# One attention-and-two-MLPs kernel: x2 added in its load buffers, the cosine's turns taken as integers, the second weights started earlier, and a new planned order

## The chip, the cores and the metric

The kernel runs on one core of a Trainium2 chip. The metric is the time of one execution on the device in microseconds (us). One execution of the kernel before was recorded by the hardware profiler; every row shown below is of that execution. TensorE is called PE here, its weight loads PEld, VectorE DVE, ScalarE ACT, GpSimd POOL, and SP is the engine whose queue issues every DMA of this kernel.

## The reference

Windowed attention (4 batches, 8 heads, 576 tokens, head size 64; half of the heads see the last 32 keys, half see 32 keys at a distance of 4) is followed by two MLPs on the 2304 tokens of 512 features:

```python
x = attn_out.transpose(0, 2, 1, 3).reshape(2304, 512)
h = x @ w_in                    # 512 -> 2048
x2 = (h * np.cos(h)) @ w_out    # 2048 -> 512
gate = 1 / (1 + np.exp(-(x2 @ w_gate)))   # 512 -> 1536
out = (gate * (x2 @ w_val)) @ w_out2      # 1536 -> 512
```

Weights of the MLPs arrive as 64-bit floats and are taken apart on the chip. Each matrix product is made of three matmuls of a high and a low part in fp32r.

## The kernel before

**Stages.** Attention (12 groups of 192 tokens) runs first, and MLP 1 is woven into it. MLP 1 works in 96 steps: 6 chunks of 384 tokens by 8 blocks of the hidden size for the first half of the hidden size (steps 0 to 47), then the 6 chunks by the other 8 blocks (steps 48 to 95). MLP 2 works in 36 sections: 3 pairs of chunks by 12 blocks; a section is seven products `p(n, j)` (a scheme that saves one product in eight) and six output groups `o(n, i)`. MLP 2's weights are prepared once, written to DRAM (`wd2`, `od2`), and loaded again for each section, so its first pair of chunks runs while later weights are still being prepared.

**One step of MLP 1.** PE makes h in PSUM (12 matmuls, L676 to L678). `turn` (ACT, L725) computes u = h/2pi + 1/4, `whole` (DVE, L729) rounds u to r by adding and subtracting a large number, `part` (DVE, L732) takes u - r, `cosine` (ACT, L735) is the sine of that times 2pi, `g` (DVE, L738) multiplies with h and frees h's PSUM buffer (there are two), `g_hi` (L743 on DVE or L745 on ACT) and `g_lo` (DVE, L748) split the product, and 12 matmuls add it to four accumulators `acc`.

**x2.** At the end of a chunk's first half the four accumulators go to DRAM (`x2h`); at the end of its second half `x2_load` (L797) brings each back into a buffer `xr` (two of them), `take` (DVE, L803) adds the accumulator into a buffer `o` (two of them), and `x2_save` (L817) writes it (`x2d`). In MLP 2 the sums `u2`, `u3` (DVE, L998) also live in `o`; `u2` must be there before product 3 of its section, `u3` before product 5, and `keep` (ACT, L995) before product 2.

**Weights.** `w_tasks(i)` for the 68 weight blocks: load (SP), `low` (ACT, L330), `mag` (L334 on DVE, L338 on ACT for the first 16 blocks), `clamp`, `shift`, `top`, `rnd` (DVE), then high and low parts; blocks i >= 32 are those of MLP 2. `block_tasks` makes `th` (ACT, L429; one buffer), which is free again once `w2_save` (L437) has landed in `wd`. L965 loads it back. There are two `raw` and two `wc` buffers for weights in work.

**What sets the order.** `Plan.run` is a list scheduler that runs at build time: each task has an engine, an assumed duration, a priority, tasks that it needs, buffers that it takes and gives, and for DMAs an assumed latency `lat` (ns) until the data are there. What it finds is written out as the program, and on the chip every engine and the SP queue work through their instructions strictly in that order. A `gate` keeps a load from being placed before PE has reached a step. [...]

Of the kernel before, what the change touches and what calls it, by code (L numbers as in the profile page):

```python
# [22 lines left out]
NEG = -(2.0**33)  # L23
MAGIC = 1.5 * 2.0**23
INV_2PI = 0.15915494309189535
TWO_PI_DOWN = 6.2831850051879883
F64_MIN = 2.0**-15
# [11 lines left out]
W_PRIO, W_START = 4.5, -4  # L39
W_GATE = (4.413, 1.646, 1.612)  # L40
XS_LEAD = (15.0, 0.6)
# [6 lines left out]
class Plan:  # L48
# [129 lines left out]
def windowed_attention_mlp_kernel(ctx, tc, q, k, v, w_in, w_out, w_gate, w_val, w_out2, out):  # L178
# [128 lines left out]
    def w_tasks(i):  # L307
# [401 lines left out]
    def mlp_tasks(n):  # L709
# [13 lines left out]
        def turn():  # L723
            st["u"] = gp.tile([P, CH], F32, tag="u", name="u")
# [6 lines left out]
        def part():  # L731
# [24 lines left out]
        for kk in range(KD):  # L756
# [9 lines left out]
        add(("turn", n), "act", 460, turn, [("h", n, KD - 1)], p - URGENT, take=["u"])  # L766
        add(("whole", n), "dve", 270, whole, [("turn", n)], p - URGENT, take=["r"], port=True)
        add(("part", n), "dve", 470, part, [("whole", n)], p - URGENT, give=["r"], port=True)
        add(("cos", n), "act", 415, cosine, [("part", n)], p - URGENT, table="trig")
# [22 lines left out]
    def x2_out(s, c, half, n, i):  # L792
        st = {}

        def load():
            st["r"] = gp.tile([P, CH], F32, tag="xr", name="xr")
            SP.dma_start(out=st["r"], in_=x2h[c][:, i, :])  # L797

        def take():
            st["o"] = gp.tile([P, CH], F32, tag="o", name="o")  # L800
            ps = acc_t[s, i][:, :CH]
            if half:
                DVE.tensor_tensor(out=st["o"], in0=ps, in1=st["r"], op=ALU.add)  # L803
            elif i % 2:
                DVE.tensor_copy(st["o"], ps)
            else:
                ACT.activation(out=st["o"], in_=ps, func=AF.Copy)

        p = n + 2.0
        deps = [("x2", n, i)]  # L810
        if half:
            add(("x2_load", s, i), "sp", 550, load, [("x2_save", order.index(c), i)], p - 4, take=["xr"], lat=2200,
                after=xr_prev("x2_load", s, i))
            deps.append(("x2_load", s, i))
        add(("x2_take", s, i), "dve" if half or i % 2 else "act", 470, take, deps, p, take=["o"],
            give=["acc"] + (["xr"] if half else []))
        add(("x2_save", s, i), "sp", 550, lambda: SP.dma_start(out=(x2d if half else x2h)[c][:, i, :], in_=st["o"]),  # L817
            [("x2_take", s, i)], p, give=["o"], lat=2200)

# [11 lines left out]
    def xs_tasks(s):  # L831
# [7 lines left out]
        for kk in range(2):  # L839
# [18 lines left out]
            def key(what, nm):  # L858
                return (what, s, kk, nm)
# [4 lines left out]
            for i, nm in enumerate(("b0", "b1", "a0", "a1")):  # L864
                c, k = (2 * s if nm[0] == "a" else 2 * s + 1), 2 * int(nm[1]) + kk
                deps = [("x2_save", NC + c, k), "late"]
                add(key("xs_load", nm), "sp", 550, lambda nm=nm, f=load: f(nm), deps, base - 1 + i * 0.01, take=["xt"], lat=2200, gate=gate,
                    after=prev + ([key("xs_load", ("b0", "b1", "a0")[i - 1])] if i else []))
# [21 lines left out]
    def xs_wide(s, ca, cb):  # L890
# [67 lines left out]
    def mlp2_tasks(n):  # L958
# [196 lines left out]
```

## Time and profile before

| what | value |
|---|---|
| median of 3 runs | 1016.99 us (1014.67 to 1018.88) |
| the profiled execution | 1018.92 us |
| its span, first to last instruction | 1017.0 us |
| PE busy, DVE busy, ACT busy | 962.0, 726.4, 473.5 us |
| weight loads of PE busy | 898.8 us |
| mean granted clock of PE | 0.98 |

The span is the part of an execution in which instructions run; 1.9 us lie around it. Busy times overlap, since the engines work side by side. Matmuls are pipelined, so PE counts as busy also where its matmuls follow each other more slowly than they could.

### The profile page before, as it was taken

What the parts mean: (1) busy time and instruction counts of PE and PEld (TensorE: products, weight loads), DVE (VectorE), ACT (ScalarE), POOL (GpSimd) and SP (SyncE); (2) the same over time, 40 slices, a digit from 0 to 9 for tenths busy, and PEclk for the clock granted to TensorE, in tenths of its full rate; (3) what the DMA queues carried; (4) which work ended last, traced back from release to release, by engine and by line L of the source; (5) the groups of instructions that cost most, each with busy time, mean ns of one, the idle gap of its engine ahead of it and who ended that gap; (6) DMA issues with size and microseconds to landing.
All of it is one profiled execution on the core that took longest, in us unless ns stands there. A gap on an engine that the chain in (4) does not pass through costs nothing.

```text
span 1017.0 us, 16393 instructions
## 1 busy us (share of the span) xinstructions
PE 962.0 (95%) x6007; PEld 898.8 (88%) x6007; DVE 726.4 (71%) x1543; ACT 473.5 (47%) x1165; POOL 184.3 (18%) x227
## 2 busy tenths in 40 slices
PE   7889999999999999999998979989999999999996
PEld 6778789898999999989998968879999999999995
DVE  7799898989865588889999777766644545543443
ACT  5768778777664254544564523332322213322112
POOL 6324333323111022222112222220000000000000
PEclk9689999999999999999999999989999999999999
DMA  7564555454310228768647889888454643644441
GB/s 185 140 183 132 170 142 175 136 168 122 77 52 7 73 88 297 272 218 280 256 178 248 295 320 341 300 309 311 175 182 171 243 151 145 212 170 186 147 145 62
DMA packets 107759, 189.80 MB, mean 187 GB/s; under 512 B 56992, under 2 KB 91040, under 8 KB 100512
## 3 DMA queue, kind: packets, MB, share of 16 engines
q1 hardware_dynamic: 107680, 188.77, 54.9%
q8 instruction: 47, 0.77, 0.3%
q14 instruction: 32, 0.26, 0.1%
HBM read 139.98 MB, written 48.76 MB: 186 GB/s over the span
## 4 chain that ended last, share of the span: by engine, by line
PE 64%; DVE 17%; DMA 10%; ACT 7%; issue 2%; SPq 0%; POOL 0%; DVEq 0%; ACTq 0%; POOLq 0%
PE oacc L1066 4%; PE oacc L1067 4%; PE oacc L1065 4%; PE acc L676 4%; PE ps_h L676 4%; PE ps_h L678 4%; PE ps_h L677 4%; PE acc L678 4%; PE acc L677 4%; PE ps_y L986 3%; PE ps_y L988 3%; PE ps_y L987 3%; DMA wd<-th 2%; PE ps_z L988 2%; PE ps_z L987 2%; PE ps_x L986 2%
## 5 line engine op out<-in xcount | busy, mean ns | idle before, releaser
L676 PE MATMUL ps_h<-arena 128*128 128x384 f32 x384 | 134.0, 349 | 5.6 <-DVE u L738 5.6
L676 PE MATMUL acc<-gs,arena 128*128 128x384 f32 x384 | 135.3, 352 | 3.8 <-DVE o L803 3.6
L678 PE MATMUL ps_h<-arena 128*128 128x384 f32 x384 | 129.7, 338 | 0.0
L677 PE MATMUL ps_h<-arena 128*128 128x384 f32 x384 | 129.7, 338 | 0.0
L678 PE MATMUL acc<-gs,arena 128*128 128x384 f32 x384 | 128.8, 335 | 0.0
L677 PE MATMUL acc<-gs,arena 128*128 128x384 f32 x384 | 128.6, 335 | 0.0
L998 DVE TENSOR_TENSOR u<-ps_y,s 128x384 f32<-128x384 f32 x72 | 39.9, 554 | 87.1 <-PE ps_y L988 80.6
L434 POOL TENSOR_TENSOR th<-tb,th 128x512 fp32r<-128x512 f32 (+1 forms) x48 | 63.6, 1343 | 211.6 <-ACT th L429 211.6
L725 ACT ACTIVATE u<-ps_h,q 128x384 f32<-128x384 f32 x96 | 55.3, 576 | 69.8 <-PE ps_h L678 51.1
L1065 PE MATMUL oacc<-arena 128*128 128x512 f32 x216 | 85.5, 396 | 2.2 <-DVE arena L1027 2.2
L1067 PE MATMUL oacc<-arena 128*128 128x512 f32 x216 | 86.5, 400 | 0.0
L1066 PE MATMUL oacc<-arena 128*128 128x512 f32 x216 | 86.4, 400 | 0.0
L676 PEld LDWEIGHTS ps_h<-arena 128*128 128x128 f32 x384 | 73.1, 190 | 9.1 <-DVE u L738 8.2
L1013 ACT ACTIVATE sg<-sg 128x384 f32<-128x384 f32 x36 | 18.8, 523 | 133.7 <-DVE sg L1009 133.7
L986 PE MATMUL ps_y<-arena 128*128 128x384 f32 x216 | 73.6, 341 | 7.3 <-DVE u L998 6.8
L676 PEld LDWEIGHTS acc<-gs,arena 128*128 128x128 f32 x384 | 72.2, 188 | 6.6 <-DVE o L803 5.3
L677 PEld LDWEIGHTS ps_h<-arena 128*128 128x128 f32 x384 | 73.2, 191 | 0.0
L988 PE MATMUL ps_y<-arena 128*128 128x384 f32 x216 | 73.1, 338 | 0.0
L987 PE MATMUL ps_y<-arena 128*128 128x384 f32 x216 | 73.1, 338 | 0.0
L678 PEld LDWEIGHTS ps_h<-arena 128*128 128x128 f32 x384 | 73.0, 190 | 0.0
L677 PEld LDWEIGHTS acc<-gs,arena 128*128 128x128 f32 x384 | 72.3, 188 | 0.0
L678 PEld LDWEIGHTS acc<-gs,arena 128*128 128x128 f32 x384 | 72.1, 188 | 0.0
(135 smaller groups left out, 2341.6 us busy)
## 6 DMA issues: line engine op xcount, KB each, us to landing
arena<-wd SPq DMA_DIRECT2D x36, 1792.0 KB, 7.4
wd<-th SPq DMA_DIRECT2D x12, 1792.0 KB, 8.4
wst<-in_moe_w_out_dram SPq DMA_DIRECT2D x28, 512.0 KB, 4.8
wst<-in_moe_w_in_dram SPq DMA_DIRECT2D x16, 512.0 KB, 4.2
xd<-arena SPq DMA_DIRECT2D x4, 1536.0 KB, 6.8
wst<-in_moe_w_gate_dram SPq DMA_DIRECT2D x12, 512.0 KB, 5.8
wst<-in_moe_w_val_dram SPq DMA_DIRECT2D x12, 512.0 KB, 4.4
arena<-xd SPq DMA_DIRECT2D x4, 1536.0 KB, 8.2
```

Source lines behind the costliest of these rows:

```text
L434: POOL.tensor_tensor(out=t[:, 1, c], in0=wf[f][:, c].bitcast(F32), in1=t[:, 0, c].bitcast(F32), op=ALU.subtract)
L676: PE.matmul(ps, wh, xl, start=first, stop=False)
L677: PE.matmul(ps, wl, xh, start=False, stop=False)
L678: PE.matmul(ps, wh, xh, start=False, stop=last)
L725: ACT.activation(out=st["u"], in_=st["h"], func=AF.Identity, scale=INV_2PI, bias=q25)
L986: PE.matmul(st[to], wh, xl, start=first, stop=False, **more)
L987: PE.matmul(st[to], wl, xh, start=False, stop=False, **more)
L988: PE.matmul(st[to], wh, xh, start=False, stop=kk == 1, **more)
L998: DVE.tensor_tensor(out=tile_of(nm, tag), in0=st[ps], in1=st[other], op=ALU.add)
L1065: PE.matmul(ps, ul, w[:, 0, :], start=f == 0, stop=False)
L1066: PE.matmul(ps, uh, w[:, 1, :], start=False, stop=False)
L1067: PE.matmul(ps, uh, w[:, 0, :], start=False, stop=f == F2 - 1)
```

## The change

- **The turns.** `turn` writes r as 32-bit integers straight from ACT; `whole` is gone; `part` is one scalar_tensor_tensor that reads h from PSUM again: u = h * (1/2pi) - r. The quarter turn moves to `cosine`, which now has a bias tile `half_pi`.
- **x2 in place.** `x2_load` of second-half chunks goes to `xr` for columns 0 and 1 and to `o` for columns 2 and 3 (all four to `xr` in the last chunk); `take` adds the accumulator into that same buffer, which is free again when the save has landed.
- **MLP 2.** `u3` uses the second half of the gate tile `sg`, `va` overwrites `u2`.
- **Weights.** MLP 2's loads may start at step 36 with 1.7 steps between them (before: 48 and 1.612). `mag` of every weight may go to ACT.
- **Assumed latencies** of weight, x2, xs, xw, `w2` and `o2` DMAs are longer.

```diff
-W_GATE = (4.413, 1.646, 1.612)
+W_GATE = (4.413, 1.646, 36.0, 1.7)
...
-            gate = min(NC * FN[0] + j * W_GATE[2], need - 8)
-        add(("w_load", i), "sp", 1460, load, [], pr - 2 if j + 2 * F1 >= 2 * FN[0] else GS * (i / 4 - 6) + W_START, take=["raw"], lat=2200, gate=gate,
+            gate = min(W_GATE[2] + j * W_GATE[3], need - 8)
+        add(("w_load", i), "sp", 1460, load, [], pr - 2 if j + 2 * F1 >= 2 * FN[0] else GS * (i / 4 - 6) + W_START, take=["raw"], lat=2200 if i < 2 * FN[0] else 3200, gate=gate,
...
-            alt=("act", 520, mag_act, False) if i < 2 * FN[0] else None)
+            alt=("act", 520, mag_act, False))
...
-        add(("o2_save", f), "sp", 1460, save, [("w_lo", i)], pr + 0.5, give=["oh"], lat=2200)
-        add(("w", key), "sp", 1460, load, [("o2_save", f), last_use(old)], NSTEP + SEC * f - 1.0, lat=2200)
+        add(("o2_save", f), "sp", 1460, save, [("w_lo", i)], pr + 0.5, give=["oh"], lat=6000)
+        add(("w", key), "sp", 1460, load, [("o2_save", f), last_use(old)], NSTEP + SEC * f - 1.0, lat=4500)
...
-        add(("w2_save", f), "sp", 4400, save, done, pr, give=["th"], lat=2200)
+        add(("w2_save", f), "sp", 5400, save, done, pr, give=["th"], lat=3500)
...
         def turn():
-            st["u"] = gp.tile([P, CH], F32, tag="u", name="u")
-            ACT.activation(out=st["u"], in_=st["h"], func=AF.Identity, scale=INV_2PI, bias=q25)
-
-        def whole():
-            st["r"] = gp.tile([P, CH], F32, tag="r", name="r", bufs=1)
-            DVE.tensor_scalar(st["r"], st["u"], MAGIC, -MAGIC, op0=ALU.add, op1=ALU.add)
+            st["r"] = gp.tile([P, CH], I32, tag="r", name="r", bufs=1)
+            ACT.activation(out=st["r"], in_=st["h"], func=AF.Identity, scale=INV_2PI, bias=q25)
 
         def part():
-            DVE.tensor_tensor(out=st["u"], in0=st["u"], in1=st["r"], op=ALU.subtract)
+            st["u"] = gp.tile([P, CH], F32, tag="u", name="u")
+            DVE.scalar_tensor_tensor(st["u"], st["h"], INV_2PI, st["r"], op0=ALU.mult, op1=ALU.subtract)
 
         def cosine():
-            ACT.activation(out=st["u"], in_=st["u"], func=AF.Sin, scale=TWO_PI_DOWN)
+            ACT.activation(out=st["u"], in_=st["u"], func=AF.Sin, scale=TWO_PI, bias=half_pi)
...
+        tag = "xr" if half and (i < 2 or s == 2 * NC - 1) else "o"
         def load():
-            st["r"] = gp.tile([P, CH], F32, tag="xr", name="xr")
-            SP.dma_start(out=st["r"], in_=x2h[c][:, i, :])
+            st["o"] = gp.tile([P, CH], F32, tag=tag, name=tag)
+            SP.dma_start(out=st["o"], in_=x2h[c][:, i, :])
 
         def take():
...
-                DVE.tensor_tensor(out=st["o"], in0=ps, in1=st["r"], op=ALU.add)
+                DVE.tensor_tensor(out=st["o"], in0=ps, in1=st["o"], op=ALU.add)
...
-        add(("u3", n), "dve", 560, lambda: plus("u3", "o", "y", "s1"), [("p", n, 3, 1), ("u2", n)], u, take=["o"])
-        add(("vb", n), "dve", 560, lambda: plus("vb", "u", "z", "u3"), [("p", n, 4, 1), ("u3", n)], u, take=["u"], give=["o"])
+        add(("u3", n), "dve", 560, lambda: plus("u3", None, "y", "s1"), [("p", n, 3, 1), ("u2", n), ("sig_a", n)], u)
+        add(("vb", n), "dve", 560, lambda: plus("vb", "u", "z", "u3"), [("p", n, 4, 1), ("u3", n)], u, take=["u"])
...
-        add(("w2", n), "sp", 4400, w_load, deps, p - 2 * SEC, take=["w2"], lat=2200)
+        add(("w2", n), "sp", 5400, w_load, deps, p - 2 * SEC, take=["w2"], lat=3500)
```

Since a planner makes the order, the diff alone doesn't show it. **DVE during attention,** some steps into MLP 1 (`ps_h` is h, `ktp` and `qbp` are keys and queries, `rs` softmax sums, `gs` the split g); before:

```order
L748 TENSOR_TENSOR gs<-u,gs 128x384
L548 COPY qbp<-ps_t 64x192 x2
L729 TENSOR_SCALAR r<-u 128x384
L548 COPY ktp_141<-ps_t 128x192
L732 TENSOR_TENSOR u<-u,r 128x384
L589 TENSOR_SCALAR rs<-rs 128x3
```

and at the same place of the changed program:

```order
L748 TENSOR_TENSOR gs<-u,gs 128x384
L550 COPY qbp<-ps_t 64x192 x2
L732 SCALAR_TENSOR_TENSOR u<-ps_h,r 128x384
L550 COPY ktp_142<-ps_t 128x192
L591 TENSOR_SCALAR rs<-rs 128x3
```

One of two instructions is gone, the other reads PSUM, and the neighbours stand as they did.

**The SP queue from the end of the second half's fourth chunk** (`x2d_76`; the next chunk's first half is `x2h_83`; `wst` are weights in work, `od` output weights of MLP 2); before:

```order
L403 DMA od_107<-oh 128x1024
L326 DMA wst<-in_moe_w_out_dram 128x1024
L323 DMA wst<-in_moe_w_gate_dram 128x4x256
L797 DMA xr<-x2h_82 128x384 x2
L817 DMA x2d_76<-o 128x384 x4
L797 DMA xr<-x2h_83 128x384 x2
```

and in the changed program:

```order
L325 DMA wst<-in_moe_w_val_dram 128x4x256
L819 DMA x2d_76<-xr 128x384 x2
L328 DMA wst<-in_moe_w_out_dram 128x1024
L819 DMA x2d_76<-o 128x384 x2
L798 DMA xr<-x2h_83 128x384 x2
L798 DMA o<-x2h_83 128x384 x2
```

Before, two of a chunk's four loads stood right ahead of its saves, and the next chunk's first two behind them; now all four loads of the next chunk stand behind this chunk's saves, each into the buffer that such a save empties.

**The SP queue where MLP 1 ends and MLP 2 begins** (`x2d_78` and `x2h_84` are the last chunk's, `wd_92` and following are section weights, loaded to `arena` and saved from `th`); before:

```order
L797 DMA xr<-x2h_84 128x384
L965 DMA arena<-wd_93 128x3584
L797 DMA xr<-x2h_84 128x384
L817 DMA x2d_78<-o 128x384 x2
L437 DMA wd_98<-th 128x3584
L817 DMA x2d_78<-o 128x384
L403 DMA od_110<-oh 128x1024
```

and in the changed program:

```order
L439 DMA wd_99<-th 128x3584
L409 DMA arena<-od_110 128x1024
L325 DMA wst<-in_moe_w_gate_dram 128x4x256
L967 DMA arena<-wd_92 128x3584
L405 DMA od_111<-oh 128x1024
L819 DMA x2d_78<-xr 128x384 x2
L325 DMA wst<-in_moe_w_val_dram 128x4x256
L328 DMA wst<-in_moe_w_out_dram 128x1024
L798 DMA xr<-x2h_84 128x384 x2
L967 DMA arena<-wd_93 128x3584
```

The last chunk's loads of columns 2 and 3 now stand behind the saves of columns 0 and 1, whose buffers they fill, and ahead of section 2's weights (`wd_93` is the second in this list of section weights). Block `wd_99` is saved here, where it was `wd_98`, so the preparation is one block further on.

## Rows read from the trace of the kernel before

**Rows 1.** The page's first line.

```profile
span 1017.0 us, 16393 instructions
```

**Rows 2.** By stretch: busy PE, PEld, DVE, ACT, POOL (instructions), clock, DMA, GB/s.

```profile
50.00:150.00 100.00, 90.59 (x725) 80.56 (x723) 91.86 (x226) 77.93 (x232) 35.44 (x49) 0.95 0.58 160
150.00:250.00 100.00, 96.66 (x786) 89.43 (x785) 88.92 (x219) 74.06 (x227) 28.99 (x44) 1.00 0.54 153
...
350.00:400.00 50.00, 50.00 (x291) 49.92 (x290) 42.03 (x87) 24.24 (x46) 11.87 (x9) 1.00 0.44 165
400.00:575.00 175.00, 166.45 (x941) 162.35 (x940) 156.73 (x319) 86.09 (x167) 38.41 (x28) 1.00 0.69 244
575.00:700.00 125.00, 111.82 (x552) 101.17 (x551) 87.67 (x168) 43.04 (x84) 31.11 (x24) 0.96 0.86 315
700.00:1000.00 300.00, 300.00 (x1561) 279.09 (x1560) 148.40 (x266) 77.86 (x152) 0.00 (x0) 1.00 0.48 177
```

**Rows 3.** PE's waits, 350 to 575 us, on whom: us, times, longest.

```profile
PE ps_h L676 <- DVE u L738: 4.8, 5, 2.5
PE acc L676 <- DVE o L803: 3.6, 2, 2.1
```

**Rows 4.** PE's waits from 575 to 700 us.

```profile
PE ps_y L986 <- DVE u L998: 6.8, 3, 5.4
PE ps_x L986 <- ACT s L995: 5.1, 2, 3.0
```

**Rows 5.** DVE, timeline: start, us, instruction, idle before it and its releaser.

```profile
590.38 0.56 DVE L998 TENSOR_TENSOR u<-ps_y,s 128x384 f32<-128x384 f32 x1 [2.78 <-DMA x2d<-o]
```

**Rows 6.** SP's queue, timeline: the issue of the save waited for.

```profile
582.72 1.02 SPq L817 DMA_DIRECT2D x2d<-o  x2
```

**Rows 7.** ACT, timeline: the instructions that stand ahead of `keep`.

```profile
626.82 1.15 ACT L429 ACTIVATE th<-tb 128x512 fp32r<-128x512 f32 x2 [2.77 <-DMA wd<-th]
...
677.82 1.15 ACT L429 ACTIVATE th<-tb 128x512 fp32r<-128x512 f32 x2 [3.60 <-DMA wd<-th]
```

**Rows 8.** DVE's groups by line: count, busy us, mean ns, idle us before.

```profile
L732 DVE TENSOR_TENSOR u<-u,r 128x384 f32<-128x384 f32 x96 | 59.3, 618 | 0.8
L738 DVE TENSOR_TENSOR u<-ps_h,u 128x384 f32<-128x384 f32 x96 | 52.7, 550 | 11.3 <-ACT u L735 10.8
...
L729 DVE TENSOR_SCALAR r<-u 128x384 f32<-128x384 f32 x96 | 38.8, 404 | 22.1 <-ACT u L725 21.6
```

**Rows 9.** `whole` (L729) alone, by stretch: DVE busy us (instructions), clock, DMA.

```profile
50.00:150.00 100.00, 5.65 (x13) 0.95 0.58 160
150.00:250.00 100.00, 5.58 (x15) 1.00 0.54 153
350.00:575.00 225.00, 20.02 (x49) 1.00 0.64 227
```

**Rows 10.** ACT's groups by line.

```profile
L725 ACT ACTIVATE u<-ps_h,q 128x384 f32<-128x384 f32 x96 | 55.3, 576 | 69.8 <-PE ps_h L678 51.1 <-DVE gs L748 15.1 <-PE ps_t L527 1.8
L735 ACT ACTIVATE u<-u 128x384 f32<-128x384 f32 x96 | 49.8, 521 | 42.9 <-DVE u L732 42.6
L330 ACT ACTIVATE wst<-wst 128x512 int32<-128x512 uint32 x68 | 46.1, 678 | 41.3 <-DMA wst<-in_moe_w_val_dram 14.4 <-DMA wst<-in_moe_w_out_dram 10.9 <-DMA wst<-in_moe_w_gate_dram 9.1
...
L365 ACT ACTIVATE arena<-wc 128x512 fp32r<-128x512 f32 x32 | 20.2, 630 | 5.5 <-DVE wc L358 5.2
...
L807 ACT ACTIVATE o<-acc 128x384 f32<-128x384 f32 x12 | 5.8, 484 | 1.8 <-DMA x2h<-o 1.7
```

**Rows 11.** The chain that ended last, 50 to 150 us, by line.

```profile
by line: DVE u L732 5.9%; DVE wc L342 5.4%; PE ps_h L676 4.6%; DVE wc L348 4.3%; DVE wc L358 4.2%; DMA wst<-in_moe_w_in_dram 4.2%; DVE rs L589 4.2%; DVE r L729 3.5%; PE ps_h L678 3.4%; PE ps_h L677 3.3%; DVE gs L748 3.3%; PE ps_s L562 3.3%;
```

**Rows 12.** DMA issues: KB each, median us from issue to landing.

```profile
wd<-th SPq DMA_DIRECT2D x12, 1792.0 KB, 8.4
...
xr<-x2h SPq DMA_DIRECT2D x24, 192.0 KB, 3.6
x2d<-o SPq DMA_DIRECT2D x24, 192.0 KB, 3.9
```

More of the change, by code (lines that the diff above doesn't have):

```diff
@@ L23 @@
 NEG = -(2.0**33)
-MAGIC = 1.5 * 2.0**23
 INV_2PI = 0.15915494309189535
-TWO_PI_DOWN = 6.2831850051879883
+TWO_PI = 6.283185307179586
+HALF_PI = 1.5707963267948966
 F64_MIN = 2.0**-15
@@ L251, in windowed_attention_mlp_kernel @@
     q25 = cst.tile([P, 1], F32, name="q25")
+    half_pi = cst.tile([P, 1], F32, name="half_pi")
     ident = ac.tile([P, P], F32, name="ident")
@@ L279, in windowed_attention_mlp_kernel @@
     POOL.memset(q25, 0.25)
+    POOL.memset(half_pi, HALF_PI)
     wseq_a = []
@@ L765, in mlp_tasks @@
                 lat=130 if kk == KD - 1 else 0, step=n if kk == 0 else None)
-        add(("turn", n), "act", 460, turn, [("h", n, KD - 1)], p - URGENT, take=["u"])
-        add(("whole", n), "dve", 270, whole, [("turn", n)], p - URGENT, take=["r"], port=True)
-        add(("part", n), "dve", 470, part, [("whole", n)], p - URGENT, give=["r"], port=True)
+        add(("turn", n), "act", 460, turn, [("h", n, KD - 1)], p - URGENT, take=["r"])
+        add(("part", n), "dve", 480, part, [("turn", n)], p - URGENT, take=["u"], give=["r"])
         add(("cos", n), "act", 415, cosine, [("part", n)], p - URGENT, table="trig")
@@ L793, in x2_out @@
         st = {}
+        tag = "xr" if half and (i < 2 or s == 2 * NC - 1) else "o"
         def load():
-            st["r"] = gp.tile([P, CH], F32, tag="xr", name="xr")
-            SP.dma_start(out=st["r"], in_=x2h[c][:, i, :])
+            st["o"] = gp.tile([P, CH], F32, tag=tag, name=tag)
+            SP.dma_start(out=st["o"], in_=x2h[c][:, i, :])
         def take():
-            st["o"] = gp.tile([P, CH], F32, tag="o", name="o")
             ps = acc_t[s, i][:, :CH]
             if half:
-                DVE.tensor_tensor(out=st["o"], in0=ps, in1=st["r"], op=ALU.add)
-            elif i % 2:
+                DVE.tensor_tensor(out=st["o"], in0=ps, in1=st["o"], op=ALU.add)
+                return
+            st["o"] = gp.tile([P, CH], F32, tag="o", name="o")
+            if i % 2:
                 DVE.tensor_copy(st["o"], ps)
@@ L811, in x2_out @@
         if half:
-            add(("x2_load", s, i), "sp", 550, load, [("x2_save", order.index(c), i)], p - 4, take=["xr"], lat=2200,
+            add(("x2_load", s, i), "sp", 550, load, [("x2_save", order.index(c), i)], p - 4, take=[tag], lat=3200,
                 after=xr_prev("x2_load", s, i))
             deps.append(("x2_load", s, i))
-        add(("x2_take", s, i), "dve" if half or i % 2 else "act", 470, take, deps, p, take=["o"],
-            give=["acc"] + (["xr"] if half else []))
+        add(("x2_take", s, i), "dve" if half or i % 2 else "act", 470, take, deps, p, take=[] if half else ["o"],
+            give=["acc"])
         add(("x2_save", s, i), "sp", 550, lambda: SP.dma_start(out=(x2d if half else x2h)[c][:, i, :], in_=st["o"]),
-            [("x2_take", s, i)], p, give=["o"], lat=2200)
+            [("x2_take", s, i)], p, give=[tag], lat=3200 if half else 2200)
     order2 = order[NC:]
@@ L866, in xs_tasks @@
                 deps = [("x2_save", NC + c, k), "late"]
-                add(key("xs_load", nm), "sp", 550, lambda nm=nm, f=load: f(nm), deps, base - 1 + i * 0.01, take=["xt"], lat=2200, gate=gate,
+                add(key("xs_load", nm), "sp", 550, lambda nm=nm, f=load: f(nm), deps, base - 1 + i * 0.01, take=["xt"], lat=4200, gate=gate,
                     after=prev + ([key("xs_load", ("b0", "b1", "a0")[i - 1])] if i else []))
@@ L927, in xs_wide @@
             deps = [("x2_save", NC + 2 * s + i, k) for k in range(KD)] + ["late", ("w2_save", F2 - 1)]
-            add(("xw_load", s, i), "sp", 1500, lambda i=i: load(i), deps + ([("xw_load", s, 0)] if i else []), base - 1, take=[] if i else ["th"], lat=2200, gate=base - 2)
+            add(("xw_load", s, i), "sp", 1500, lambda i=i: load(i), deps + ([("xw_load", s, 0)] if i else []), base - 1, take=[] if i else ["th"], lat=6000, gate=base - 2)
         loads = [("xw_load", s, 0), ("xw_load", s, 1)]
@@ L997, in plus @@
         def plus(nm, tag, ps, other):
-            DVE.tensor_tensor(out=tile_of(nm, tag), in0=st[ps], in1=st[other], op=ALU.add)
+            if nm == "u3":
+                st[nm] = new_sg()[:, 1, :]
+            elif nm == "va":
+                st[nm] = st[other]
+            else:
+                tile_of(nm, tag)
+            DVE.tensor_tensor(out=st[nm], in0=st[ps], in1=st[other], op=ALU.add)
         def new_sg():
@@ L1046, in mlp2_tasks @@
         add(("sig_a", n), "act", 370, sig_a, [("p", n, 2, 1)], u, take=["gs"], give=["h"], table="sig")
-        add(("u3", n), "dve", 560, lambda: plus("u3", "o", "y", "s1"), [("p", n, 3, 1), ("u2", n)], u, take=["o"])
-        add(("vb", n), "dve", 560, lambda: plus("vb", "u", "z", "u3"), [("p", n, 4, 1), ("u3", n)], u, take=["u"], give=["o"])
-        add(("gate_b", n), "dve", 560, gate_b, [("p", n, 5, 1), ("sig_a", n)], u, give=["h", "r"])
+        add(("u3", n), "dve", 560, lambda: plus("u3", None, "y", "s1"), [("p", n, 3, 1), ("u2", n), ("sig_a", n)], u)
+        add(("vb", n), "dve", 560, lambda: plus("vb", "u", "z", "u3"), [("p", n, 4, 1), ("u3", n)], u, take=["u"])
+        add(("gate_b", n), "dve", 560, gate_b, [("p", n, 5, 1), ("vb", n)], u, give=["h", "r"])
         add(("sig_b", n), "act", 415, sig_b, [("gate_b", n)], u, table="sig")
-        add(("va", n), "dve", 560, lambda: plus("va", "u", "z", "u2"), [("p", n, 6, 1)], u, take=["u"], give=["h", "o"])
+        add(("va", n), "dve", 560, lambda: plus("va", None, "z", "u2"), [("p", n, 6, 1)], u, give=["h"])
         free = [("o", n - 2, TT * 2 - 1)] if n >= 2 else [("h", NSTEP - 1, KD - 1)]
@@ L1055, in mlp2_tasks @@
             add(("u_hi", n, i), "act", 415, lambda i=i: u_hi(i), [("mul", n, i)] + free, u)
-            add(("u_lo", n, i), "dve", 560, lambda i=i: u_lo(i), [("u_hi", n, i)], u, give=["u"], port=True)
+            add(("u_lo", n, i), "dve", 560, lambda i=i: u_lo(i), [("u_hi", n, i)], u, give=["u" if i else "o"], port=True)
         add(("sg_free", n), None, 0, nothing, [("mul", n, 0), ("mul", n, 1)], u, give=["gs"])
```

2 lines of the change are left out of this document (1 added, 1 removed).

## The prediction

> **What bounds the kernel now.** The profiled execution took 1018.92 us, 1.9 of them around its span [rows 1], and 1.9 above the median of the runs; the sum below is made against 1018.92 and moved by that at the end. PE is the engine to keep busy: nothing else is close to full after attention. I first cut the busy time by stretch [rows 2]. A busy share hides matmuls that follow each other too slowly, so I count them instead. From 350 to 400 us PE is never idle and starts 291 matmuls, 171.8 ns each; that is MLP 1's pace. From 700 to 1000 it starts 1561, 192.2 ns each; that is MLP 2's. At these paces the 941 matmuls of 400 to 575 us need 161.7 us of 175: 13.3 are lost (the idle time alone would say 8.6). The 552 matmuls of 575 to 700 need 106.1 of 125: 18.9 lost. After 700 us there is nothing to win. During attention the matmuls differ too much to be counted; there PE is idle for 9.4 us of 50 to 150 and for 3.3 of 150 to 250, while DVE is busy for 92 and 89 us. So attention is near DVE's limit and the middle has losses that waits must explain.
>
> Next I read who PE waits for. From 350 to 575 us it waits 4.8 us for `g` (L738), which frees h's buffer, and 3.6 us in two waits for x2's `take` (L803) [rows 3]. From 575 to 700 it waits 6.8 us for the sums u2 and u3 (L998) and 5.1 us for `keep` (L995) [rows 4]; the granted clock is 0.96 there, so 0.04 x 125 = 5.0 us go with the clock, which can be the higher level or half of it; about 2.0 of the 18.9 are left for the rest. The two waits can be traced back. The sum at 590.38 was held by a landing x2 save [rows 5] that SP issued at 582.72 [rows 6]: 7.7 us, because the sum needs an `o` buffer. `keep` stood behind ACT instructions that waited 2.8 and 3.6 us for the landing of a `th` save [rows 7], which has one buffer.
>
> **The turns.** `whole` (404 ns) goes; `part` changes from 618 ns to a two-input instruction with a PSUM operand [rows 8]. That form isn't in the trace. The nearest is `g` (L738), also PSUM with SBUF, 128x384: 550 ns; the upper end is today's 618, as nothing suggests more. I take 550, since shape and operands are those. DVE then saves 404 + 618 - 550 = 472 ns a step, 45 us over 96 steps. On ACT, `cosine` gets a bias tile. `turn` has one and takes 576 ns from PSUM, a plain copy from PSUM 484 [rows 10]: +92 ns, so 521 becomes 613. The integer output of `turn` costs between nothing and 48 ns, what the integer instruction L330 (678) has over L365 (630) at equal size [rows 10]; I take nothing, as L330 also reads with a stride.
>
> [...]
>
> Where does the saving count? Between 50 and 150 us the chain that ended last has `whole` for 3.5% and `part` for 5.9% [rows 11] of 100 us. Without the first, and with the second shortened by 68/618, it is 4.1 us shorter; 13 steps [rows 9] of 92 ns on ACT are 1.2 us, half of which I put on the chain: 3.5 us. Between 150 and 250 us DVE saves 15 x 0.472 = 7.1 us, but PE is idle only 3.3; I take half of that, 1.5. **Term 1: 5 us**, bounds 0 (ACT or PE takes over at once; ACT is busy for 78 of 100 us) and 28 x 0.472 = 13.2.
>
> **The middle, 350 to 575 us.** DVE is busy for 199 of 225 us [rows 2]; 49 steps [rows 9] save 23 us of it. Some of `mag` moves to ACT, which is busy for 110 of 225. The 3.6 us of `take` go: as the order rows show, all four loads of a chunk are issued behind the chunk before, some seven steps early, in place of right before use. Of the 4.8 us for `g` I take half, of the 4.9 that no wait names a third: with a tenth of DVE's work gone its queue is shorter, but PE's order has the same depth. **Term 2: 3.6 + 2.4 + 1.5 = 7.5 us**, bounds 0 and 13.3.
>
> **The seam, 575 to 700 us.** u3 no longer lies in `o` and the last chunk's x2 doesn't either, so u2 and u3 can't wait for an x2 save: 6.8 us go. In their place a wait appears. The last chunk's loads of columns 2 and 3 stand in SP's queue behind the landing of saves 0 and 1; DVE has their two `take`s ahead of the next u3, and PE needs the third accumulator for an output group. Counting PE's order of the changed program from the first `take` to that group, there are 18 products of three matmuls (9.3 us at 171.8 ns) and two output groups (1.2 at 192.2): 10.4 us of cover. The new chain is a save, a load and a `take`: at the worst save seen 7.7 + 3.6 + 0.55 = 11.9, at median landings 3.9 + 3.6 + 0.55 = 8.1 [rows 12]. So 0 to 1.5 us, and behind these loads stands section 2's weight load; I take 2. For `th` the planner now assumes 8.9 us from issue to landing (5400 + 3500 ns) in place of 6.6; the median is 8.4 [rows 12]. Its user is placed some 2.3 us later each time, up to 4.6 of the 5.1 us; I take 3, as other blocks can meet late saves. The clock's 5.0 us come with these waits: (4.8 + 3)/11.9 of it is 3.3; I take 2.7. **Term 3: 4.8 + 3 + 2.7 = 10.5 us**, bounds 0 and 16.9.
>
> The earlier start has no term of its own. Until attention's buffers are free only two more blocks can be loaded, at the cost of two `low` on ACT (678 ns each [rows 10]), covered while ACT is half busy. At MLP 1's end the order is one block of twelve ahead, which eases DMA (share 0.86 in the seam [rows 2]) without ending it.
>
> **Sum:** 5 + 7.5 + 10.5 = 23 us; 1018.9 - 23 = 995.9, and 1.9 less for the median: **994 us**.
>
> **Rivals.**
> *Relief hidden* (17%). ACT's longer cosine and exp batches hold attention where it is, and DVE's time in the middle was slack: then term 1 is 0, term 2 the 3.6 of `take`, term 3 half, 5: 8.6, so 1008. For it: ACT at 78%. Against: DVE at 92%, and its share of the chain [rows 11].
> *Part is no shorter* (8%): at 618 ns the saving is 404 a step; term 1 becomes 4.3, term 2 6.9, the sum 21.7 and the time 995. [...]
> *Given back at SP, no change* (7%), and *slower* (6%), one mechanism at two sizes. Loads into a buffer that a save must first empty hold SP's queue until it lands, and the next weight blocks stand behind them, then DVE's weight instructions, then `g` for PE. There are six such places, one a chunk. At the median landing, 3.9 us, wholly exposed, they cost 23.4 us, which eats the gain: 1017. At 5.8, midway to the worst of 7.7, they cost 34.8: 1029. Slower is decided from (23 + 5)/6 = 4.7 us each. Against both: the planner lays the loads early, two raw buffers cover one late weight block, and before SP also waited for buffers there.
> *As forecast* (62%), 994, by itself 984 to 1005.
>
> **Numbers.** A change under 0.5% (5 us) can't be told from none here. As forecast, *no shorter* and *hidden* are faster: 0.87; same 0.07; slower 0.06. The range leaves out *slower*, *given back* and some 5 in 100 of the forecast's far side: 980 (a gain of 37 us, where all upper bounds together are 43) to 1013.
>
> **What would show it.** Right: no L729 group, `part` at about 550 ns and `cosine` at about 613; DVE busy some 45 us less; PE idle from 50 to 250 us down by about 5; no wait of PE for `take` between 350 and 575 us; from 575 to 700 us no DVE sum that waits for an x2 save, at most 3 us for a late x2 load, and a granted clock above 0.96. Wrong: `part` above 618; the idle time in attention unchanged with ACT ahead of it; SP waiting several us at each chunk's end with PE idle behind it; or the `th` wait as long as now at another block.

## The result: 983.5 us, 3.3% faster than before

The changed kernel takes 983.46 us (median of 4 runs, 982.42 to 986.80); before, 1017.93 on the same chip. The ratio is 0.967, 95% interval 0.9635 to 0.9705. That is 34 us, where 23 were forecast (994 us, range 980 to 1013). The signs of all three terms were right and each was too small. The experiments show that a part of the third term cannot be credited to the cause that it was given, and that the earlier start, which got no term at all, is the part that costs most when it is undone.

The first lines of the profile after, and its stretches (columns as in [rows 2]):

```profile
span 981.6 us, 16366 instructions
...
PE 950.2 (97%) x6007; PEld 893.0 (91%) x6007; DVE 688.8 (70%) x1419; ACT 494.8 (50%) x1193; POOL 177.2 (18%) x228
```

```profile
50.00:150.00 100.00, 92.14 (x754) 83.05 (x754) 92.17 (x229) 81.25 (x234) 36.53 (x52) 0.98 0.57 168
150.00:250.00 100.00, 97.88 (x806) 90.32 (x805) 87.32 (x211) 75.21 (x229) 30.00 (x47) 1.00 0.49 144
...
400.00:550.00 150.00, 149.50 (x863) 149.11 (x862) 129.21 (x246) 91.85 (x173) 37.16 (x29) 1.00 0.76 264
550.00:667.00 117.00, 115.30 (x598) 106.09 (x597) 76.36 (x143) 40.49 (x78) 19.99 (x16) 1.00 0.83 302
667.00:967.00 300.00, 300.00 (x1561) 279.25 (x1560) 148.16 (x266) 78.27 (x152) 0.00 (x0) 1.00 0.46 169
```

The two stretches with losses in [rows 2] are now almost full. In 400 to 550 us, 863 matmuls at MLP 1's 171.8 ns need 148.3 of 150 us; in 550 to 667, 598 at MLP 2's 192.2 ns need 114.9 of 117. Together 4 us are lost where 32 were, and the granted clock is 1.00 through both. Attention still has DVE at 92% and PE with gaps.

1.00 is the higher of the two levels of the granted clock in these two traces, 0.50 the lower. In the seam of before it was below 1.00 twice, each time where one of PE's two longest waits there ended (5.41 us at 591.00, 3.02 at 679.81). From 680 to 686 us PE was never idle and started a matmul every 375 ns at 0.50; from 688 on it was one every 188 ns at 1.00:

```profile
590.00:594.00 4.00, 3.00 (x9) 2.71 (x10) 1.66 (x3) 0.00 (x0) 0.00 (x0) 0.57 0.97 410
680.00:686.00 6.00, 6.00 (x16) 5.13 (x17) 3.12 (x7) 2.17 (x5) 3.34 (x3) 0.50 0.66 279
688.00:700.00 12.00, 12.00 (x64) 11.20 (x63) 5.88 (x12) 2.86 (x6) 1.29 (x1) 1.00 0.75 270
```

PE's waits between 350 and 667 us answer to [rows 3] and [rows 4]:

```profile
PE ps_x L988 <- DVE u L1006: 0.6, 1, 0.6
PE ps_y L988 <- DVE u L738: 0.5, 1, 0.5
PE oacc L1073 <- DVE xr L803: 0.5, 1, 0.5
PE ps_y L988 <- DVE u L1006: 0.2, 1, 0.2
PE ps_x L988 <- ACT s L997: 0.2, 1, 0.2
PE oacc L1073 <- DVE arena L1035: 0.2, 1, 0.2
PE ps_h L678 <- DVE u L738: 0.2, 1, 0.2
```

No wait is over 0.6 us; before, the longest was 5.4. The groups of the turns, by line, answer to [rows 8] and [rows 10]:

```profile
L732 DVE SCALAR_TENSOR_TENSOR u<-ps_h,r 128x384 f32<-128x384 f32 x96 | 52.8, 550 | 14.6 <-ACT r L728 13.8
```

```profile
L735 ACT ACTIVATE u<-u,half_pi 128x384 f32<-128x384 f32 x96 | 58.5, 612 | 38.5 <-DVE u L732 37.8
L728 ACT ACTIVATE r<-ps_h,q 128x384 int32<-128x384 f32 x96 | 55.4, 577 | 58.3 <-PE ps_h L680 55.8 <-PE ps_p L602 1.6 <-PE ps_t L529 0.6
```

`part` takes 550 ns (forecast 550), `cosine` 612 (613), the integer output costs 1 ns over 576. One sign missed: DVE is busy 37.6 us less (726.4 to 688.8) and not 45, although the groups of the turns alone fell by 45.3 us; where the rest went was not followed up.

**Where the time came from.** PE's timeline gives the start of each step and section (12 h matmuls a step, 12 `ps_x` matmuls a section). From these starts, us in each stage of one profiled execution:

| kernel | steps 0-47 and before | steps 48-95 | sections 0-11 | median of its runs |
|---|---|---|---|---|
| before | 354.7 | 211.8 | 160.3 | 1017.9 |
| changed | 346.6 | 200.1 | 144.8 | 983.5 |
| only_turns | 348.4 | 206.8 | 154.5 | 1002.6 |
| only_buffers | 351.6 | 203.3 | 153.7 | 1002.1 |
| only_start | 352.2 | 213.4 | 159.4 | 1017.9 |
| only_latencies | 349.6 | 210.0 | 175.1 | 1025.8 |
| pair | 354.4 | 209.6 | 151.0 | 1006.7 |
| no_turns | 352.0 | 203.3 | 143.4 | 992.2 |
| no_buffers | 349.2 | 204.0 | 151.3 | 995.6 |
| no_start | 350.7 | 200.4 | 166.5 | 1005.8 |
| no_latencies | 350.7 | 204.5 | 147.4 | 1000.0 |
| no_save_latency | 347.2 | 200.5 | 142.8 | 982.7 |
| extra_dve | 352.9 | 201.7 | 144.3 | 990.6 |

So attention and MLP 1's first half gave 8.1 us, its second half 11.7, the first twelve sections 15.5: 35.3 of the 35.4 by which the two profiled executions differ. The first column wants care: only_buffers is instruction for instruction the kernel before through the whole of attention, and still its profile is 3.1 us ahead there. The granted clock (the third number from the end) differs by about as much. The first row is the kernel before, whose row from 50 to 150 us is in [rows 2] with 0.95; the other two are only_buffers:

```profile
0.00:50.00 50.00, 39.29 (x388) 35.57 (x389) 36.95 (x95) 31.81 (x103) 25.00 (x56) 0.83 0.65 162
```

```profile
0.00:50.00 50.00, 38.06 (x405) 33.98 (x406) 37.96 (x98) 32.78 (x107) 25.01 (x56) 0.86 0.70 168
50.00:150.00 100.00, 89.45 (x717) 79.39 (x717) 94.16 (x230) 78.69 (x234) 35.75 (x49) 0.97 0.57 159
```

0.03 of 50 us and 0.02 of 100 us make an estimated 3.5 us. The changed kernel has 0.83 and 0.98 in these two stretches, so an estimated 3 of its 8.1 us in this column are clock and some 5 are left. In the seam the clock went from 0.96 over 125 us to 1.00, another 5 us. So an estimated 8 of the 35.4 us go with the granted clock. A difference of 3 us in the first column is one execution against another; the last column decides.

### The profile page after: what moved, and what is told of

Same layout as the page of the kernel before. It is cut to its first block, busy times and chain, and to the rows that moved or that the text cites. A ratio compares the mean times of both kernels' runs of the same rounds, so it can differ in the third digit from the quotient of the medians.

```text
span 981.6 us, 16366 instructions
## 1 busy us (share of the span) xinstructions
PE 950.2 (97%) x6007; PEld 893.0 (91%) x6007; DVE 688.8 (70%) x1419; ACT 494.8 (50%) x1193; POOL 177.2 (18%) x228
## 4 chain that ended last, share of the span: by engine, by line
PE 73%; DVE 12%; DMA 7%; ACT 6%; issue 2%; SPq 1%; ACTq 0%; DVEq 0%
PE acc L678 5%; PE ps_h L678 5%; PE oacc L1074 5%; PE oacc L1075 5%; PE oacc L1073 5%; PE acc L680 4%; PE acc L679 4%; PE ps_h L680 4%; PE ps_h L679 4%; PE ps_y L988 3%; PE ps_y L990 3%; PE ps_y L989 3%; PE ps_z L990 2%; PE ps_z L989 2%; PE ps_z L988 2%; PE ps_x L988 2%
## 5 line engine op out<-in xcount | busy, mean ns | idle before, releaser
L678 PE MATMUL ps_h<-arena 128*128 128x384 f32 x384 | 131.8, 343 | 0.2 <-DVE u L738 0.2
L679 PE MATMUL ps_h<-arena 128*128 128x384 f32 x384 | 128.9, 336 | 0.0
L680 PE MATMUL ps_h<-arena 128*128 128x384 f32 x384 | 128.8, 335 | 0.0
L436 POOL TENSOR_TENSOR th<-tb,th 128x512 fp32r<-128x512 f32 (+1 forms) x48 | 60.4, 1272 | 185.4 <-ACT th L431 152.9
L1073 PE MATMUL oacc<-arena 128*128 128x512 f32 x216 | 84.5, 391 | 2.4 <-DVE arena L1035 1.9
L1075 PE MATMUL oacc<-arena 128*128 128x512 f32 x216 | 85.5, 396 | 0.0
L1074 PE MATMUL oacc<-arena 128*128 128x512 f32 x216 | 85.5, 396 | 0.0
L728 ACT ACTIVATE r<-ps_h,q 128x384 int32<-128x384 f32 x96 | 55.4, 577 | 58.3 <-PE ps_h L680 55.8
L735 ACT ACTIVATE u<-u,half_pi 128x384 f32<-128x384 f32 x96 | 58.5, 612 | 38.5 <-DVE u L732 37.8
L1006 DVE TENSOR_TENSOR sg<-ps_y,s 128x384 f32<-128x384 f32 x36 | 20.0, 556 | 80.3 <-PE ps_y L990 80.3
L678 PEld LDWEIGHTS acc<-gs,arena 128*128 128x128 f32 x384 | 72.2, 188 | 0.9
L679 PEld LDWEIGHTS acc<-gs,arena 128*128 128x128 f32 x384 | 72.3, 188 | 0.0
```

Source lines behind the costliest of these rows:

```text
L436: POOL.tensor_tensor(out=t[:, 1, c], in0=wf[f][:, c].bitcast(F32), in1=t[:, 0, c].bitcast(F32), op=ALU.subtract)
L678: PE.matmul(ps, wh, xl, start=first, stop=False)
L679: PE.matmul(ps, wl, xh, start=False, stop=False)
L680: PE.matmul(ps, wh, xh, start=False, stop=last)
L728: ACT.activation(out=st["r"], in_=st["h"], func=AF.Identity, scale=INV_2PI, bias=q25)
L1073: PE.matmul(ps, ul, w[:, 0, :], start=f == 0, stop=False)
```

## The experiments

The change has four separable parts: the turns; the buffers (x2 in place, u3 and va, with the x2 DMAs' own latencies); the start (gate and `mag` on ACT); the latencies (all other `lat` numbers). Each was tried alone on the kernel before, and undone alone in the changed kernel. The planner lays the order anew for every run, so a run shows a part together with the order that it brings, and the gains of parts need not add up. Runs were made on different chips, on which the kernel before had medians of 1017.25 to 1017.93 us; undone parts are set against the changed kernel's 983.46. Theory A: each part helps in its own stage. Theory B: DVE's relief does it all. Theory C: the assumed latencies do most.

### Each part alone

**only_turns**, the turns' lines of the diff ahead, with their tasks for the planner, and nothing else:

```diff
...
-        add(("turn", n), "act", 460, turn, [("h", n, KD - 1)], p - URGENT, take=["u"])
-        add(("whole", n), "dve", 270, whole, [("turn", n)], p - URGENT, take=["r"], port=True)
-        add(("part", n), "dve", 470, part, [("whole", n)], p - URGENT, give=["r"], port=True)
+        add(("turn", n), "act", 460, turn, [("h", n, KD - 1)], p - URGENT, take=["r"])
+        add(("part", n), "dve", 480, part, [("turn", n)], p - URGENT, take=["u"], give=["r"])
```

> The kernel before with the turns alone (integers from ACT, no rounding on DVE, part from PSUM, cosine with a bias). Theory A, each edit in its own stage: attention ends 8 us earlier as in the changed kernel, about half of the middle's loss goes, the seam's waits for x2 saves and for the th save stay: 12 to 18 us faster than before, near 1002. Theory B, it is all DVE's time: a DVE with 45 us less work absorbs the waits of the middle and the seam too: 25 us or more, below 993. Theory C, the assumed latencies do most: 8 to 10 us, all of it in attention, near 1009.

Measured: 1002.58 us, ratio 0.9838 (0.9802 to 0.9873): 15 us, as theory A had it. The seam keeps waits for u2 and u3 (L997); `keep`'s is not there. PE from 575 to 720 us:

```profile
PE ps_y L985 <- DVE u L997: 4.8, 2, 4.4
PE ps_x L985 <- DVE sg L1008: 2.7, 1, 2.7
```

**only_buffers**, x2 in place and MLP 2's tiles:

```diff
...
-            st["r"] = gp.tile([P, CH], F32, tag="xr", name="xr")
-            SP.dma_start(out=st["r"], in_=x2h[c][:, i, :])
+            st["o"] = gp.tile([P, CH], F32, tag=tag, name=tag)
+            SP.dma_start(out=st["o"], in_=x2h[c][:, i, :])
...
+            if nm == "u3":
+                st[nm] = new_sg()[:, 1, :]
...
```

> The kernel before with the buffers alone (x2 in place in its load buffers, u3 in the gate tile, va over u2, with the x2 DMAs' own longer latencies). Theory A: the 3.6 us of waits for take in the middle and 7 to 8 us at the seam's start go, attention is unchanged: 8 to 12 us faster, near 1007. Theory B: under 4 us, since DVE is as full as before. Theory C: 3 to 6 us.

Measured: 1002.10 us, ratio 0.9836 (0.9794 to 0.9878): 16 us, more than any theory gave. The wait for u2 and u3 is gone at the seam; `keep` is what is left:

```profile
PE ps_x L989 <- ACT s L998: 5.1, 3, 2.5
PE oacc L1074 <- DVE arena L1036: 0.4, 1, 0.4
```

**only_start:**

```diff
-W_GATE = (4.413, 1.646, 1.612)
+W_GATE = (4.413, 1.646, 36.0, 1.7)
...
-            alt=("act", 520, mag_act, False) if i < 2 * FN[0] else None)
+            alt=("act", 520, mag_act, False))
```

> The kernel before with the earlier start of the second weights alone (gate 36 and 1.7, mag also on ACT). Theory A: attention unchanged, a part of the seam's DMA crowd gone, 0 to 6 us faster, near 1014. Theory B: mag on ACT takes some 10 us off DVE, so 3 to 6 us. Theory C: within 3 us of before either way, as the late landings stay unplanned for.

Measured: 1017.88 us, ratio 1.0002 (0.9980 to 1.0025): nothing. Theory C holds, and the low end of A; B misses.

**only_latencies**, all other longer latencies (two of them here):

```diff
...
-        add(("w2_save", f), "sp", 4400, save, done, pr, give=["th"], lat=2200)
+        add(("w2_save", f), "sp", 5400, save, done, pr, give=["th"], lat=3500)
...
-        add(("w2", n), "sp", 4400, w_load, deps, p - 2 * SEC, take=["w2"], lat=2200)
+        add(("w2", n), "sp", 5400, w_load, deps, p - 2 * SEC, take=["w2"], lat=3500)
```

> The kernel before with the longer assumed latencies of weight, o2, w2, xs and xw DMAs alone. Theory A: the waits of keep behind the th save (5.1 us and their clock) go, with little else: 5 to 9 us faster, near 1010. Theory B: under 3 us. Theory C: most of the middle's 13 and the seam's 19 us go: 18 us or more, below 1000.

Measured: 1025.83 us, ratio 1.0063 (1.0029 to 1.0098): 8 us slower, and all three theories fall. By the table the first twelve sections take 14.8 us longer, the stages before them 6.9 us less, 5.1 of it before step 48 (the longer landing is assumed for weight blocks from 16 on, so it acts in attention too). PE's timeline at the start of section 11, and SP's ahead of it:

```profile
717.55 0.69 PE L986 MATMUL ps_x<-arena 128*128 128x384 f32 x1 [8.38 <-DMA arena<-wd]
```

```profile
696.91 0.32 SPq L437 DMA_DIRECT2D wd<-th  x1
703.12 0.32 SPq L965 DMA_DIRECT2D arena<-wd  x1
703.48 0.43 SPq L900 DMA_DIRECT2D xw<-x2d  x1
703.96 0.43 SPq L965 DMA_DIRECT2D arena<-wd  x1
```

These four in the program (`wd_91` is the first of the twelve blocks, `wd_102` the last):

```order
L437 DMA wd_102<-th 128x3584
L965 DMA arena<-wd_91 128x3584
L900 DMA xw<-x2d_75 128x1536
L965 DMA arena<-wd_102 128x3584
```

The last block is saved at 696.91 us, 11.7 later than before (685.22). It is loaded back from 703.96, and ahead of it in the queue stand the 1792 KB of section 12's weights and 768 KB of x2, though section 11 comes first on PE. Section 11's weights end PE's wait 13.6 us after their issue; the median of all these loads in this run is 7.6 us. Section 11 waits 8.4 us, PE's longest wait after attention in any run here, and the granted clock is 0.70 in the 17.5 us that follow:

```profile
arena<-wd SPq DMA_DIRECT2D x36, 1792.0 KB, 7.6
```

```profile
717.50:735.00 17.50, 13.19 (x49) 12.29 (x50) 10.27 (x17) 8.48 (x14) 0.00 (x0) 0.70 0.35 130
```

Of all the programs here only this one and no_start have section 12's weights ahead of section 11's. Why the planner lays the last save later was not followed up; the longer assumed landings are the only edit.

### Each part undone

**no_turns:**

```diff
...
-        add(("turn", n), "act", 460, turn, [("h", n, KD - 1)], p - URGENT, take=["r"])
-        add(("part", n), "dve", 480, part, [("turn", n)], p - URGENT, take=["u"], give=["r"])
+        add(("turn", n), "act", 460, turn, [("h", n, KD - 1)], p - URGENT, take=["u"])
+        add(("whole", n), "dve", 270, whole, [("turn", n)], p - URGENT, take=["r"], port=True)
+        add(("part", n), "dve", 470, part, [("whole", n)], p - URGENT, give=["r"], port=True)
```

> The changed kernel with the turns undone (rounding on DVE again, part from SBUF, cosine without bias); all else as changed. Theory A: attention's 8 us come back and about half of the middle's 12: near 1000 (14 to 18 us slower than the changed kernel). Theory B: most of the gain goes, near 1010. Theory C: only attention's 8 us come back, near 992.

Measured: 992.16 us, 8.7 slower than the changed kernel; by the table 5.4 before step 48, 3.2 after it, none in the sections. That is C's number; A's 14 to 18 and B fall.

**no_buffers:**

```diff
...
-            st["o"] = gp.tile([P, CH], F32, tag=tag, name=tag)
-            SP.dma_start(out=st["o"], in_=x2h[c][:, i, :])
+            st["r"] = gp.tile([P, CH], F32, tag="xr", name="xr")
+            SP.dma_start(out=st["r"], in_=x2h[c][:, i, :])
...
```

> The changed kernel with the buffers undone (x2 loads to xr and sums to o, u3 and va in tiles of their own). Theory A: waits for take and for an x2 save come back, 8 to 12 us slower than the changed kernel, near 994. Theory B: under 4 us slower, as DVE has time to catch up. Theory C: under 4 us slower, as the planner lays the sums later.

Measured: 995.59 us, 12 slower, as A had it. The wait for u2 is back at 6.7 us:

```profile
PE ps_y L985 <- DVE u L997: 6.7, 1, 6.7
```

**no_start:**

```diff
...
-            gate = min(W_GATE[2] + j * W_GATE[3], need - 8)
+            gate = min(NC * FN[0] + j * W_GATE[2], need - 8)
...
```

> The changed kernel with MLP 2's weights starting at step 48 again and their mag on DVE. Theory A: the seam's DMA crowd and the last blocks come back, 3 to 8 us slower than the changed kernel, near 989. Theory B: 2 to 5 us, from mag on DVE. Theory C: under 3 us, since the late landings are planned for.

Measured: 1005.79 us, 22 slower, nearly three times what any theory gave. PE from 575 to 720 us has the late last block again, with section 12's weights ahead of section 11's in the queue as in only_latencies:

```profile
PE ps_x L988 <- DMA arena<-wd: 8.0, 1, 8.0
PE oacc L1073 <- DVE arena L1035: 7.2, 3, 4.3
```

**no_latencies:**

```diff
-        add(("w_load", i), "sp", 1460, load, [], pr - 2 if j + 2 * F1 >= 2 * FN[0] else GS * (i / 4 - 6) + W_START, take=["raw"], lat=2200 if i < 2 * FN[0] else 3200, gate=gate,
+        add(("w_load", i), "sp", 1460, load, [], pr - 2 if j + 2 * F1 >= 2 * FN[0] else GS * (i / 4 - 6) + W_START, take=["raw"], lat=2200, gate=gate,
...
-        add(("w2_save", f), "sp", 5400, save, done, pr, give=["th"], lat=3500)
+        add(("w2_save", f), "sp", 4400, save, done, pr, give=["th"], lat=2200)
...
```

> The changed kernel with the old assumed latencies of weight, o2, w2, xs and xw DMAs. Theory A: the waits behind th come back, 5 to 9 us slower than the changed kernel, near 991. Theory B: under 3 us. Theory C: most of the middle's and the seam's gain goes, 18 us or more, above 1001.

Measured: 999.98 us (994.63 to 1000.53; the profiled one is the 994.63), 16 slower, between A and C and nearer to C. ACT waits for weights to land, ahead of the step's own instructions in its order:

```profile
ACT wst L332 <- DMA wst<-in_moe_w_val_dram: 13.1, 7, 5.1
ACT wst L332 <- DMA wst<-in_moe_w_out_dram: 9.3, 9, 2.3
ACT wst L332 <- DMA wst<-in_moe_w_gate_dram: 6.3, 5, 2.9
```

That is 28.7 us; before, the same three are 34.4 [rows 10]. In the changed kernel they are 13.3:

```profile
ACT wst L332 <- DMA wst<-in_moe_w_gate_dram: 7.2, 4, 4.9
...
ACT wst L332 <- DMA wst<-in_moe_w_val_dram: 3.7, 4, 1.5
ACT wst L332 <- DMA wst<-in_moe_w_out_dram: 2.4, 4, 1.1
```

That these waits make the 16 us is argued, not shown: the profiled execution is only 11.1 us slower than the changed kernel's, 4.1 of them before step 48.

### Start and latencies together, and what each is made of

Nothing alone, and minus 8 alone, yet 22 and 16 when undone: theory D, that these two are one edit.

**pair**, the kernel before with the diffs of only_start and only_latencies.

> The kernel before with both the earlier start and the longer assumed latencies, turns and buffers as before. Alone, the start gave nothing and the latencies cost 8 us. Theory D, the two are one edit in two parts (longer latencies make the planner lay a block's steps further apart, so the last blocks come too late unless the chain starts earlier; an earlier start without them puts instructions ahead of data that have not landed): 10 to 18 us faster than before, near 1004, with no wait for a section's weights. Rival, effects that add: 8 us slower, near 1026. Second rival, the pair needs the turns' free DVE time or the buffers as well: within 5 us of before.

Measured: 1006.70 us, ratio 0.9901 (0.9865 to 0.9936), 10.5 us faster where the sum of the two alone is 8 slower. No section waits for its weights any more; the seam's wait for u2, which the buffers cure, stays (7.0 us). Theory D stands, at its low end.

**no_save_latency:**

```diff
-        add(("o2_save", f), "sp", 1460, save, [("w_lo", i)], pr + 0.5, give=["oh"], lat=6000)
-        add(("w", key), "sp", 1460, load, [("o2_save", f), last_use(old)], NSTEP + SEC * f - 1.0, lat=4500)
+        add(("o2_save", f), "sp", 1460, save, [("w_lo", i)], pr + 0.5, give=["oh"], lat=2200)
+        add(("w", key), "sp", 1460, load, [("o2_save", f), last_use(old)], NSTEP + SEC * f - 1.0, lat=2200)
...
-        add(("w2_save", f), "sp", 5400, save, done, pr, give=["th"], lat=3500)
+        add(("w2_save", f), "sp", 4400, save, done, pr, give=["th"], lat=2200)
```

> The changed kernel with the old assumed latencies for the saves of prepared weights and the out2 reload alone (w2_save, o2_save, w out2); weight loads, w2, xs and xw keep the longer ones. Undoing all of them cost 16 us. Theory D1, the one buffer th and its save are what ACT stumbles over: 8 to 16 us slower than the changed kernel, near 996. Rival, the weight loads' 3.2 us are what counts: under 4 us slower, near 985.

Measured: 982.66 us, no different from the changed kernel. D1 falls: in the changed kernel the latency of the saves is worth nothing. ACT waits 4.0 us for `th` here, and PE loses nothing by it (its longest wait from 350 to 720 us is 0.5):

```profile
ACT wst L332 <- DMA wst<-in_moe_w_out_dram: 6.2, 4, 4.3
...
ACT th L431 <- DMA wd<-th: 4.0, 4, 1.5
ACT wst L332 <- DMA wst<-in_moe_w_val_dram: 3.9, 5, 1.7
```

So the 16 us of no_latencies need what no_save_latency kept: weight loads, w2, xs and xw. Which of these four is not told apart, nor whether the saves count once these are undone; the waits of `low` point to the weight loads.

**extra_dve**, the removed rounding's time without its place in the chain:

```diff
+        def again():
+            DVE.tensor_scalar(st["u"], st["u"], 1.0, 0.0, op0=ALU.mult, op1=ALU.add)
...
-        add(("g_lo", n), "dve", 470, g_lo, [("g_hi", n)], p - URGENT, give=["u"], port=True)
+        add(("g_lo", n), "dve", 470, g_lo, [("g_hi", n)], p - URGENT, port=True)
+        add(("again", n), "dve", 270, again, [("g_lo", n)], p - URGENT, give=["u"], port=True)
```

> The changed kernel with one more DVE instruction a step, of the removed rounding's form and size (384 elements, one SBUF operand, in place on u after its last use), on which no other instruction of the step waits; outputs are unchanged. Undoing the turns cost 8.7 us. Theory E, DVE's time is what the turns gave: 5 to 9 us slower than the changed kernel, near 990. Rival, the shorter chain from h to its free buffer is what they gave: under 2 us slower, near 984.

Measured: 990.58 us (990.49 to 990.92), 7.1 slower. The added group has 96 instructions of 414 ns, `whole`'s 404; DVE between 150 and 250 us is at 90.5 instead of 87.3:

```profile
L751 DVE TENSOR_SCALAR u<-u 128x384 f32<-128x384 f32 x96 | 39.6, 414 | 0.7
```

```profile
150.00:250.00 100.00, 96.54 (x786) 89.36 (x786) 90.45 (x222) 75.31 (x228) 30.21 (x47) 1.00 0.53 153
```

Theory E stands: 7.1 of the 8.7 us that the turns are worth when undone come back, though no instruction of the step's chain waits for the added one. By the table 6.3 us come before step 48 and 1.6 in the steps after it.

**attn_latencies**, a try for a faster version: 3.2 us assumed for the first weights and for q, k and v.

```diff
...
-        add(("load_v", a), "sp", 900 if plain else 500, load_v, [], p2 - V_LEAD, take=["v"], lat=2200,
+        add(("load_v", a), "sp", 900 if plain else 500, load_v, [], p2 - V_LEAD, take=["v"], lat=3200,
```

> The changed kernel with longer assumed landings (3.2 in place of 2.2 us) in attention too: first weights, q, k and v loads. A try for a faster version. If the planned order stumbles over late landings there as well: 2 to 6 us faster, near 979. Rival, attention waits for DVE and ACT and not for landings: within 3 us of the changed kernel.

Measured: 984.78 us (984.29 to 985.05), not faster. A longer assumed landing of these loads gains nothing; the rival holds.

## Why the prediction was right, and where its steps failed

**The turns' prices** were right to a few ns, and so was the place: attention. Term 1 forecast 5 us; the profiles show 8.1, of which some 3 go with the granted clock; undoing the turns gives 5.4 in that stage. The cause was right too (extra_dve), though the longer latencies alone give 5.1 us there as well, for which the forecast had nothing.

**Term 2, the middle** (forecast 7.5, measured 11.7). That the loads right ahead of their use cost `take`'s waits was right: 3.6 us were forecast for the buffers, and undone alone they cost 3.9 in this stage. DVE's relief was given half of `g`'s wait and a third of the unnamed rest, 3.9 us; the turns give 3.2 undone and 5.0 alone. The step that failed is what was left out: I left 5.8 of 13.3 us to PE's own depth and put nothing on the assumed latencies, which cost 4.4 us here when undone. The start costs 0.3.

**Term 3, the seam** (forecast 10.5, measured 15.5). Each of its three sums was too small. The waits for u2 and u3 went, and the new wait for x2 is 0.5 us where I took 2; `keep`'s wait fell from 5.1 to 0.2 where I took 3 off; all 5.0 us of the clock came back where I took 2.7. The half about x2's buffers held, its working included. The last chunk's two `take`s in the changed kernel, on DVE:

```profile
556.56 0.56 DVE L803 TENSOR_TENSOR xr<-acc,xr 128x384 f32<-128x384 f32 x1 [1.07 <-PE acc L680]
...
568.17 1.01 DVE L803 TENSOR_TENSOR xr<-acc,xr 128x384 f32<-128x384 f32 x2
```

They are 11.6 us apart, against 10.4 us of cover; PE waited 0.5 (forecast 0 to 1.5, taken as 2). The half about `th` failed as a price: "its user is placed some 2.3 us later" was to take 3 us off, and no_save_latency, without that assumption, is as fast. `keep`'s wait is at most 0.4 us in every run that assumes 8.9 us, so the longer assumption is enough to remove it. But of the six programs that assume 6.6 only three have it (before and only_buffers 5.1, only_start 2.1); only_turns, no_latencies and no_save_latency have 0.3 or less. In the changed kernel it is not needed; what else moves `keep` out of the way there was not singled out.

**"The earlier start has no term of its own"** is the step that was furthest off. It read the start's effect from where it begins, and not from where the chain of twelve blocks ends: the last save goes at 639.25 us in the changed kernel and at 679.85 in no_start. Undone, it costs 22 us; with it the longer latencies are affordable, without it they make section 11 wait 8 us for its weights. That the two have to be priced together is what no row of before could show directly, but how late the last block is saved could have been read there (685.22, with section 11 at 715.3).

The rivals *given back at SP* and *slower* put the danger at the x2 loads. The danger was real at another queue entry: the last `wd` load.

## What to carry to other kernels

- Where a planner fixes the order, an assumed latency and a start time are one choice: with longer latencies the last block came so late here that the planner put the next section's weights ahead of it. So ask first whether the last link still comes in time, and read the order of the queue there.
- Price an earlier start at the end of its chain, and try edits both alone and undone: here the four alone sum to a gain of 23 us, and together they give 34.
- To tell an engine's time from a chain's length, put the removed work back where nothing waits for it.

## What was not expected of the hardware

- `part` on DVE, now with one PSUM operand, was steadier than at the same size with two SBUF operands: it went from a mean of 618 ns to 550, while `g_lo`, still on SBUF alone, stands at 640 (621 before). The medians are alike; a few long ones make the difference. `part` before, `part` and `g_lo` after (ns: shortest, median, longest):

```profile
L732 DVE TENSOR_TENSOR u<-u,r x96: 527/550/1661, 56.1 to 567.8; 128x384 f32<-128x384 f32 x96
```

```profile
L732 DVE SCALAR_TENSOR_TENSOR u<-ps_h,r x96: 526/550/559, 54.1 to 545.5; 128x384 f32<-128x384 f32 x96
L748 DVE TENSOR_TENSOR gs<-u,gs x96: 522/552/1711, 64.4 to 552.4; 128x384 fp32r<-128x384 f32 x96
```

  By the trace seven of `part`'s 96 took over 600 ns before, and each of the seven ran while POOL was busy; the 75 that ran while POOL was idle took 559 ns at most. After, 27 ran while POOL was busy, and none took longer than 559. No run takes POOL's work away, so the cause stays a reading of the trace.
- Converting to 32-bit integers on ACT's output was free: a mean of 577 ns against 576 over 96 instructions each.
- One and the same attention took 3.1 us less in another execution (351.6 against 354.7, up to step 48), with an estimated 3.5 us less lost to the lower level of the granted clock (means of 0.86 against 0.83 over the first 50 us, and 0.97 against 0.95 over the next 100).
